# Decode attention plus MLP on one core: V in 4 MB transfers, P turned whole, the MLP's first half ahead of K

## The chip, the cores and the metric

One core of a Trainium2 chip runs the whole kernel in one launch. The metric is the device time of that launch in microseconds, lower is better. Engines are called PE (matrix), DVE (vector), ACT (scalar), POOL (GpSimd) and SP (sync); SP issues nearly all DMAs here, on one queue that is served by 16 DMA engines.

## The reference

```python
xn = layernorm(A_x)                                   # A_x: 4 x 1 x 576, bf16
out = A_x + attention(xn) + mlp(xn)

# attention: B=4, Hq=32, Hkv=16 (two query heads share a KV head), Dh=128, Sk=8192
W = 2048                                              # only the last 2048 keys of the cache
q = (xn @ wq).reshape(4, 1, 32, 128)                  # wq: 576 x 4096
p = softmax(q . k[:, :, Sk-W:] * 128**-0.5)
attention = (p . v[:, :, Sk-W:]).reshape(4, 1, 4096) @ wo      # wo: 4096 x 576

# mlp: h = gelu(layernorm(xn) @ w1) (576 x 576); four channel groups of h are shifted along S,
# where S = 1, so that the shifted entries are the zero padding; hs = shifted @ w2
x1 = xn + hs
mlp = x1 + gelu(layernorm(x1) @ w3) @ w4              # w3: 576 x 4608, w4: 4608 x 576
```

K and V of the window are 33.6 MB each; all weights together are 21.5 MB. Everything is read once.

## The kernel before

Each engine's program is a list of operations with a key; the list is sorted by key and written out in that order (`emit_program`). An operation names the signals that it waits for, so the keys set the order on an engine and the waits set the dependencies between engines. SP's list is the order of the DMAs: one that waits holds back all behind it.

**K stage.** 16 chunks, each one batch entry and four KV heads (`CH`), 2 MB, in 16 KB runs, loaded into a ring of ten slots. A chunk is 128 partitions (4 heads x 32 groups of 64 keys). PE transposes 64 tiles of 128 x 128 per chunk (`pe_T`, L333), eight to a PSUM bank (three banks, `NTB`); DVE (L340) and ACT (L339, blocks `ACT_EVAC`) copy them to `ktbuf`. `pe_SC` (L351) multiplies with the query: four matmuls of 512 columns at the four column positions 0, 32, 64, 96. The sixteen of a chunk are issued together. All scores of the four PSUM banks `Sps` accumulate over the chunks, so that the 128 rows are the 128 pairs of batch and query head.

**Softmax.** DVE takes the maximum (L372), ACT the exponentials (L376). P is then masked into four copies (L384), turned in 64 small matmuls (L393), copied (L402), permuted by a matmul (L404) and copied again (L406), on ACT.

**PV stage.** V comes in 16 chunks of 2 MB like K's. For each chunk DVE builds a padded, masked slice of P (`dve_pad`, L422), and PE runs 64 matmuls with a V tile as weights and 8 columns of P (L433). After a KV group's last chunk the rows are scaled (`OTn`, L472), selected (`sel`, L449) and multiplied with wo (`pe_AO`), in three portions (`AO_CH`).

**Weights.** wq loads first and K follows. w1, w2 and wo wait for the softmax and are issued after the eighth V chunk; wo in two DMAs with 4.6 KB runs. The MLP's first half runs in the PV stage. w3 (five DMAs) and w4 (five pieces of 18, 10, 5, 2 and 1 row per partition, `W4_ROWS`) come after V and reuse the ring. The h2 product (L525, L529: 180 matmuls with w3 as strided weights) runs near the end, and then the w4 product: 36 rows in two halves of 288 columns (L456, the helper `acc_mm`), both at column position 0, added in PSUM (`ACC`) to the residual and the attention's result. `fin0` and `fin1` (L550, L551) copy the sums out, and two DMAs write them.

Of the kernel before, what the change touches and what calls it, by code (L numbers as in the profile page):

```python
# [12 lines left out]
NSLOT = 10  # L13
NKT = 12
NTB = 3
SC_LAG = 2
ACT_EVAC = (1, 4, 7)
N_WARM = 6
AO_CH = ((0, 4), (4, 6), (6, 8))
# [14 lines left out]
def bass_parallel_sum__sliding_block_cached__mixer_s_mlp__decode_kernel(  # L34
# [8 lines left out]
    NU = 4  # L43
# [11 lines left out]
    CH = [(b, gq) for gq in range(4) for b in range(B)]  # L55
    x2 = A_x.rearrange("b s d -> (b s) d")
    o2 = out.rearrange("b s d -> (b s) d")

    with ExitStack() as ctx:
# [5 lines left out]

        ring_t = sb("ring", [128, NSLOT * UE], BF16)
        regB_t = sb("regB", [128, NKT * 1024], BF16)
        PT_t = sb("PT", [128, NT * 32], BF16)
# [4 lines left out]
        P4 = regB_t[:, 0:4 * NU * 512].rearrange("p (q t u i) -> p q t u i", q=4, t=16, u=NU)  # L73
        PTx = regB_t[:, 4 * NU * 512:4 * NU * 512 + 4 * 512].rearrange("p (q x) -> p q x", q=4)
        PTpad = regB_t[:, 0:2 * NT * 2 * NU].rearrange("p (s t u e) -> p s t u e", s=2, t=NT, u=NU)
        PTv = PT_t[:].rearrange("p (t c e) -> p t c e", t=NT, c=NC)

        wqmain = ring_t[:, 8 * UE:10 * UE].rearrange("p (r n) -> p r n", r=4)
        wqrag = PT_t[:, 0:Hq * Dh // 2]
        wo_a = ring_t[:, 4 * UE:4 * UE + 7 * 4 * D].rearrange("p (h r n) -> p h r n", h=7, r=4)  # L80
        _o = 2 * NT * 2 * NU
        wo_b = regB_t[:, _o:_o + 4 * D].rearrange("p (r n) -> p r n", r=4)
        _o += 4 * D
        w1main = regB_t[:, _o:_o + 4 * D].rearrange("p (r n) -> p r n", r=4)
        _o += 4 * D
        w1rag = regB_t[:, _o:_o + HALF]
        _o += HALF
        w2main = regB_t[:, _o:_o + 4 * D].rearrange("p (r n) -> p r n", r=4)
        _o += 4 * D
        w2rag = regB_t[:, _o:_o + HALF]  # L90
        _o += HALF
        assert _o <= NKT * 1024
        wo_at = lambda hg: wo_a[:, hg] if hg < 7 else wo_b
        w3r = [ring_t[:, 6 * UE + r * F:6 * UE + (r + 1) * F] for r in range(3)] + [ring_t[:, 8 * UE:8 * UE + F]]
        w3rag = ring_t[:, 6 * UE + 3 * F:6 * UE + 3 * F + FH]
        assert 3 * F + FH <= 2 * UE
# [9 lines left out]
        x1n_bf = sb("x1n_bf", [B, D], BF16)  # L106
        ragsrc = sb("ragsrc", [B, 3, 2, 128], BF16)
# [9 lines left out]
        permT_bf = sb("permT_bf", [128, 128], BF16)  # L117
        ident_f = sb("ident_f", [128, 128], FP32)
        ones_f = sb("ones_f", [128, 128], FP32)
        mask4 = sb("mask4", [128, NU], FP32)  # L120
        sel_f = sb("sel_f", [128, 32], FP32)
        sel_bf = sb("sel_bf", [128, 32], BF16)
        mU = sb("mU", [128, NU], FP32)
        mU_bf = sb("mU_bf", [128, NU, 2], BF16)
        diag = sb("diag", [128, 128], FP32)
        zeros_bf = sb("zeros_bf", [128, 512], BF16)
# [5 lines left out]
        rinvB = sb("rinvB", [128, 128], FP32)  # L132
        P_sb = Qpad_t[:, 0:2048].rearrange("p (q x) -> p q x", q=4)
        OTn = sb("OTn", [128, 128], BF16)
        ORT = sb("ORT", [128, 4, 8, B], BF16)
        t1 = sb("t1", [B, D], FP32)
        out_sb = x1n_bf
# [4 lines left out]
        PTps = [ps[:, 4 + k, :].rearrange("p (t x) -> p t x", t=16) for k in range(4)]  # L142
        ACC = [ps[0:B, k, 0:HALF] for k in range(2)]
        ORps = ps[:, 2, 0:128].rearrange("p (r h b) -> p r h b", r=4, h=8)
        rinvps = ps[:, 3, 0:128]
        OTps = [ps[:, 6 - max(gq - 1, 0), 0:128] for gq in range(4)]
        QTps = ps[:, 7, 0:128]
        HSps = ps[0:B, 7, 128:128 + HALF]
        HTps = ps[:, 7, 416:440].rearrange("p (c b) -> p c b", b=B)
        XTps = [ps[:, 7, 440 + 12 * k:452 + 12 * k].bitcast(BF16).rearrange("p (c b) -> p c b", b=B) for k in range(3)]  # L150
        H2Tps = ps[:, 7, 0:144].rearrange("p (c b) -> p c b", b=B)
# [25 lines left out]

        KS = float(NB + 4)
# [6 lines left out]
        def pool_ident(t, tag, pattern, view, key):  # L185
# [3 lines left out]
        P(lambda e: e.memset(zeros_bf[:], 0.0), sig="zeros_bf", key=-100)  # L189
# [4 lines left out]
        pool_ident(permT_bf, "permT_bf", [[-1, NI], [-NI, NU]], permT_bf[:].rearrange("p (i u) -> p i u", u=NU), -95)  # L194
        pool_ident(ident_f, "ident_f", [[-1, 128]], ident_f[:], -94)
        P(lambda e: e.memset(hs_inT[:], 0.0), sig="hs_inT", key=-90)
        P(lambda e: e.memset(ones_f[:], 1.0), sig="ones_f", key=-89)


        add("dve", lambda e: e.tensor_reduce(out=mask4[:], in_=ident_f[:].rearrange("p (u x) -> p u x", u=NU), axis=AX.X, op=ALU.add),  # L200
            waits=["ident_f"], sig="mask4", key=-8)
        add("dve", lambda e: e.tensor_reduce(out=sel_f[:], in_=ident_f[:].rearrange("p (u x) -> p x u", u=NU), axis=AX.X, op=ALU.add),
            waits=["ident_f"], sig="sel_f", key=-8)
        add("dve", lambda e: e.tensor_copy(out=sel_bf[:], in_=sel_f[:]), waits=["sel_f"], sig="sel_bf", key=-7.9)
        add("dve", lambda e: e.tensor_reduce(out=mU[:], in_=ident_f[:].rearrange("p (i u) -> p u i", u=NU), axis=AX.X, op=ALU.add),
            waits=["ident_f"], sig="mU", key=-8)
        for x in range(2):
            add("dve", lambda e, x=x: e.tensor_copy(out=mU_bf[:, :, x], in_=mU[:]), waits=["mU"], sig=f"mU_bf{x}", key=-7.8)
# [3 lines left out]
        ev_wq = [add_dma([(ring_t[:, 8 * UE:10 * UE], A_wq[0:512, :].rearrange("(p r) n -> p (r n)", r=4))], "wq", (), -20),  # L212
                 add_dma([(wqrag, rag_src(A_wq))], "wqr", (), -15)]

        def kv_src(cache, c):
            b, gq = CH[c]
            return cache[b, NU * gq:NU * gq + NU, Sk - W:Sk, :].rearrange("g (i t) d -> i g (t d)", t=NT)

        k_slot = lambda c: c % NSLOT
        v_slot = lambda c: (6, 7, 8, 9, 0, 1, 2, 3)[c % 8]  # L220
        t_done = lambda c: f"T{NBLK * c + NBLK - 1}"
        ev_k, ev_v = [], []
        for c in range(NC):
            w = ["q"] if c in (8, 9) else ([t_done(c - NSLOT)] if c >= NSLOT else [])
            ev_k.append(add_dma([(slot(k_slot(c)), kv_src(A_k_cache, c))], ("ring", k_slot(c)), w, c))
        for c in range(NC):
            w = [f"PV{c - 8}"] if c >= 8 else [t_done(c + 6)]
            ev_v.append(add_dma([(slot(v_slot(c)), kv_src(A_v_cache, c))], ("ring", v_slot(c)), w, KS + c))
            if c == 7:
                free = ["PTy3"]  # L230
                ev_w1 = add_dma([(w1main, B_w1[0:512, :].rearrange("(p r) n -> p r n", r=4)), (w1rag, rag_src(B_w1))], "w1",
                                free, KS + c + 0.1)
                ev_w2 = add_dma([(w2main, B_w2[0:512, :].rearrange("(p r) n -> p r n", r=4)), (w2rag, rag_src(B_w2))], "w2",
                                free, KS + c + 0.2)
                wo_s = A_wo.rearrange("(h p r) n -> p h (r n)", h=8, r=4)
                ev_wo = add_dma([(wo_a.rearrange("p h r n -> p h (r n)"), wo_s[:, 0:7, :]),
                                 (wo_b.rearrange("p r n -> p (r n)"), wo_s[:, 7, :])],
                                "wo", [t_done(NC - 1)] + free, KS + c + 0.3)
        w3_src = B_w3[0:512, :].rearrange("(p r) n -> p r n", r=4)
        ev_w3 = [add_dma([(w3r[r], w3_src[:, r, :])], ("w3", r), ["PV10" if r == 3 else "PV9"], KT + r) for r in range(4)]  # L240
        ev_w3.append(add_dma([(w3rag, rag_src(B_w3))], ("w3", 4), ["PV9"], KT + 4))
        w4tile, w4cols, ev_w4, W4N = [], [], [], []
        base = 0
        offs = (8 * UE + F, 0, 10 * D, 15 * D, 17 * D)
        assert F + 18 * D <= 2 * UE and 18 * D <= 2 * UE
        for n, rc in enumerate(W4_ROWS):
            v = ring_t[:, offs[n]:offs[n] + rc * D]
            ev_w4.append(add_dma([(v, B_w4[base:base + 128 * rc, :].rearrange("(p r) n -> p (r n)", r=rc))], ("w4", n),
                                 ["PV11" if n == 0 else "PV13"], KT + 5 + n))
            W4N.append((len(w4tile), len(w4tile) + rc))  # L250
            for r in range(rc):
                w4tile.append(v[:, r * D:(r + 1) * D])
                w4cols.append((base + r, base + 128 * rc, rc))
            base += 128 * rc
        assert len(w4tile) == 36 and base == F
        ev_o = [None, None]
        for h, eng in ((0, "sp"), (1, "act")):
            ev_o[h] = add_dma([(o2[:, HALF * h:HALF * (h + 1)], out_sb[:, HALF * h:HALF * (h + 1)])], ("out", h),
                              [f"fin{h}"], 10000, engine=eng)
            add(eng, lambda e: None, [ev_o[h]], None, 10001)  # L260


        def ln_ops(idx, src, dst, first_waits, tag, k0):
# [11 lines left out]
            add("dve", lambda e: (e.tensor_copy(out=ragsrc[:, idx, 0, 0:128:2], in_=dst[:, 512:D]),  # L275
# [81 lines left out]
        for n in range(NB):  # L357
            w = [ev_k[n // NBLK]] if n % NBLK == 0 else []
            if n == 0:
                w.append("perm_bf")  # L360
# [271 lines left out]
```

## Time and profile before

| | us |
|---|---|
| median of 3 runs | 224.17 |
| lowest, highest | 224.01, 224.96 |
| the profiled execution, span from first to last instruction | 222.3 |
| PE busy | 162.3 (73%) |
| DVE busy | 76.9 (35%) |
| ACT busy | 61.2 (28%) |
| transposes of K on PE, L333 | 66.7 |
| w4 product, L456 | 11.1 |
| HBM read | 88.49 MB, 398 GB/s over the span |

The profiled execution has no time of its own in the record beside its span; the span is 1.9 us under the median of the runs, which includes what lies before the first and after the last instruction. The page's slices are 5.56 us each; a digit is the busy share in tenths. PEclk is the clock granted to PE: full until slice 19, about half from slice 20 on. In the groups, a line gives engine, operation, operands, count, then busy time, the mean duration of one in ns, and the engine's idle time ahead of it. Matmuls overlap, so the distance between two starts is shorter than the duration of one.

### The profile page before, as it was taken

Reading aid. Unit: us, or ns where it says so; the run is one execution under the profiler, and the core shown is the slowest. Engines: PE = TensorE matmul, PEld = TensorE weight load, DVE = VectorE, ACT = ScalarE, POOL = GpSimd, SP = SyncE. Lnnn points to the kernel's source line nnn. Section 1 sums busy time; section 2 is a strip of 40 time slices with the busy share of each in tenths; the row PEclk is TensorE's granted clock in tenths of the full one; section 3 lists DMA queues with packets and bytes.
Section 4 is the critical chain, followed back from the end, with each engine's and each line's share of the span. In section 5 each row is a group of like instructions: output and inputs, shape, how many; then the busy total and the mean of one; then the engine's idle time right before and its main releaser. Section 6 shows DMA issues by size and latency. Waiting matters only on the chain.

```text
span 222.3 us, 6311 instructions
## 1 busy us (share of the span) xinstructions
PE 162.3 (73%) x2964; PEld 126.4 (57%) x2966; DVE 76.9 (35%) x162; ACT 61.2 (28%) x75; POOL 5.5 (2%) x17
## 2 busy tenths in 40 slices
PE   0068999999999999995377653001948996699596
PEld 0065777777777777773257653001545584489363
DVE  4303656666666655666822111000150010000000
ACT  2000655556556665555860000000002000000000
POOL 8100000000000000000000000000000000000000
PEclk9999999999999999999655555555555697585589
DMA  7999999999999999999999999999999999999820
GB/s 284 407 410 425 436 431 419 420 428 431 428 431 422 422 431 428 423 422 422 425 428 425 433 405 401 413 438 428 428 425 419 428 431 415 421 426 428 359 109 1
DMA packets 8017, 88.90 MB, mean 400 GB/s; under 512 B 812, under 2 KB 1208, under 8 KB 3000
## 3 DMA queue, kind: packets, MB, share of 16 engines
q1 hardware_dynamic: 7976, 88.50, 94.7%
q8 instruction: 23, 0.38, 0.7%
q14 instruction: 2, 0.02, 0.0%
q10 hardware_dynamic: 16, 0.01, 0.0%
HBM read 88.49 MB, written 0.00 MB: 398 GB/s over the span
## 4 chain that ended last, share of the span: by engine, by line
DMA 56%; PE 41%; ACT 1%; issue 1%; SPq 1%; DVE 0%
DMA ring<-in_A_v_cache_dram 34%; PE ps L333 25%; DMA ring<-in_B_w_dram 16%; PE ps L351 6%; DMA ring<-in_A_wq_dram 6%; PE ps L456 5%; PE ps L304 2%; PE ps L433 2%; PE ps L321 1%; ACT regB L339 1%; SPq L171 1%; DVE Qpad L313 0%; ACT x1n_bf L551 0%; PE ps L283 0%; PE ps L286 0%
## 5 line engine op out<-in xcount | busy, mean ns | idle before, releaser
L333 PE MATMUL ps<-perm_bf,ring 128*128 128x128 bf16 x1024 | 66.7, 221 | 0.5 <-ACT regB L339 0.4
L333 PEld LDWEIGHTS ps<-perm_bf,ring 128*128 128x128 bf16 x1024 | 58.0, 98 | 13.5 <-issue 6.9
L340 DVE COPY regB<-ps 128x1024 bf16<-128x1024 bf16 x80 | 52.3, 687 | 29.9 <-PE ps L333 28.1
L339 ACT ACTIVATE regB<-ps 128x1024 bf16<-128x1024 bf16 x48 | 47.5, 1022 | 48.8 <-PE ps L333 48.8
L433 PE MATMUL ps<-regB,ring 128*128 128x8 bf16 x1024 | 29.0, 168 | 33.8 <-DMA ring<-in_A_v_cache_dram 27.8
L433 PEld LDWEIGHTS ps<-regB,ring 128*128 128x128 bf16 x1024 | 28.3, 103 | 37.1 <-issue 31.8
L351 PE MATMUL ps<-regB,Qpad 128*32 128x512 bf16 x256 | 16.9, 382 | 0.4 <-ACT regB L339 0.4
L269 ACT ACTIVATE sd<-mv 4x1 f32<-4x1 f32 x3 | 0.6, 202 | 51.1 <-DVE mv L267 51.1
L456 PE MATMUL ps<-ring,h2T_sb 128*4 128x288 bf16 x72 | 11.1, 325 | 2.3 <-DMA ring<-in_B_w_dram 2.3
L422 DVE TENSOR_TENSOR regB<-PT,mU_bf 128x512 bf16<-128x512 bf16 x16 | 6.6, 419 | 15.9 <-PE ps L433 13.8
L456 PE MATMUL ps<-ring,ORT 128*4 128x288 bf16 x56 | 11.3, 380 | 0.3 <-DVE ORT L475 0.3
L535 ACT ACTIVATE h2T_sb<-ps 128x144 bf16<-128x144 f32 x1 | 0.3, 292 | 37.3 <-PE ps L529 37.3
L456 PEld LDWEIGHTS ps<-ring,h2T_sb 128*4 128x4 bf16 x72 | 6.8, 95 | 6.3 <-DMA ring<-in_B_w_dram 2.4
L475 DVE CAST ORT<-ps 128x32 bf16<-128x32 f32 (+1 forms) x3 | 0.6, 203 | 26.7 <-PE ps L449 26.7
L550 DVE CAST x1n_bf<-ps 4x288 bf16<-4x288 f32 x1 | 0.4, 446 | 27.0 <-PE ps L456 27.0
L304 PE MATMUL ps<-xnT,ring 128*128 128x4 bf16 x128 | 3.6, 166 | 7.9 <-DMA ring<-in_A_wq_dram 7.9
L351 PEld LDWEIGHTS ps<-regB,Qpad 128*32 128x32 bf16 x256 | 5.3, 95 | 6.0 <-issue 0.9
L456 PEld LDWEIGHTS ps<-ring,ORT 128*4 128x4 bf16 x56 | 5.8, 107 | 4.5 <-DVE ORT L475 0.4
L525 PEld LDWEIGHTS ps<-x1nT,ring 128*128 128x128 bf16 x144 | 8.0, 152 | 0.2 <-issue 0.2
L525 PE MATMUL ps<-x1nT,ring 128*128 128x4 bf16 x144 | 8.1, 194 | 0.0
L304 PEld LDWEIGHTS ps<-xnT,ring 128*128 128x128 bf16 x128 | 3.5, 104 | 7.9 <-DMA ring<-in_A_wq_dram 7.9
L472 DVE TENSOR_TENSOR OTn<-ps,rinvB 128x32 bf16<-128x32 f32 (+1 forms) x3 | 0.6, 202 | 18.5 <-PE ps L433 18.5
(92 smaller groups left out, 72.3 us busy)
## 6 DMA issues: line engine op xcount, KB each, us to landing
ring<-in_A_k_cache_dram SPq DMA_DIRECT2D x16, 2048.0 KB, 43.3
ring<-in_A_v_cache_dram SPq DMA_DIRECT2D x16, 2048.0 KB, 43.1
ring<-in_B_w_dram SPq DMA_DIRECT2D x4, 1152.0 KB, 33.4
ring<-in_A_wq_dram SPq DMA_DIRECT2D x1, 4096.0 KB, 12.3
ring<-in_A_wo_dram SPq DMA_DIRECT2D x1, 4032.0 KB, 32.1
ring<-in_B_w_dram SPq DMA_DIRECT2D x1, 2592.0 KB, 36.6
ring<-in_B_w_dram SPq DMA_DIRECT2D x1, 1440.0 KB, 30.3
regB<-in_B_w_dram SPq DMA_DIRECT2D x2, 576.0 KB, 21.3
```

What stands on the lines that cost most here:

```text
L171: e.dma_start(o_, i_).then_inc(S[skey], 16)
L269: add("act", lambda e: e.activation(out=sd[:, idx:idx + 1], in_=mv[:, idx, 1:2], func=ACTF.Sqrt, bias=EPS, scale=1.0), waits=[f"{tag}_mv"] ...
L304: ins = e.matmul(QTps[:, B * h:B * (h + 1)], lhsT=w, rhs=x_, start=(r == 0 and h == 0), stop=(r == 4), skip_group_check=True)
L321: ins = e.matmul(ps[:, 4 + (w % NTB), :], lhsT=zeros_bf[:, 0:128], rhs=zeros_bf[:, :], start=True, stop=True)
L333: ins = e.transpose(tb[n % NTB][:, t, :], slot_t(k_slot(c))[:, 8 * k + t, :], perm_bf[:])
L339: return "act", lambda e: e.activation(out=ktbuf[:, n % NKT], in_=tb[n % NTB], func=ACTF.Copy)
L340: return "dve", lambda e: e.tensor_copy(out=ktbuf[:, n % NKT], in_=tb[n % NTB])
L351: ins = e.matmul(Sps[32 * u:32 * u + 32, q, :].rearrange("p (t i) -> p t i", t=16), lhsT=Qpad_t[:, qo:qo + 32], rhs=ktgrp[:, s % (NKT // 2 ...
L422: return lambda e: e.tensor_tensor(out=PTpad[:, c % 2], in0=PTv[:, :, cc, :].unsqueeze(2).to_broadcast([128, NT, NU, 2]), in1=mU_bf[:].uns ...
L433: ins = e.matmul(o_, lhsT=slot_t(v_slot(c))[:, t, :], rhs=PTpad[:, c % 2, t].rearrange("p u e -> p (u e)"), start=(t == 0), stop=(t == NT ...
L456: return e.matmul(ACC[h], lhsT=lhsT, rhs=rhs, start=start, stop=stop)
L525: ins = e.matmul(H2Tps[:, n, :], lhsT=w3r[r][:, lo:hi:st], rhs=x1nT[:, r, :], start=(r == 0 and n == 0), stop=False, skip_group_check=True)
```

## The change

- **V**: 8 transfers of 4 MB in place of 16 of 2 MB. Chunk c takes the KV heads m, m+4, m+8, m+12 (m = c // 2) of all four batch entries, and the half j = c % 2 of each run of 256 keys: 128 partitions of 32 KB runs. The last chunk comes in two halves. V uses the K ring as four slots.
- **P**: turned whole in 16 matmuls of 128 columns (`pe_PT`) and copied by DVE to `PTn`. For each V chunk, 16 matmuls of 256 columns with a 0/1 matrix `Sel` spread it over partitions (`pe_B`), and eight DVE products mask it into `PTpad` (`dve_pad`). A PV matmul has 32 columns instead of 8, and all chunks of two m share one accumulation.
- **Order**: w1, w2 and w3 load right after wq, ahead of K, into places of their own (w3: `regX`) or into the ring; the MLP up to h2 runs before the first transpose. K has a ring of 8 slots, four PSUM banks and eight places in `ktbuf`; score matmuls are issued in fours, one group for each two blocks.
- **wo**: two groups of four DMAs, each DMA for 32 partitions with 18 KB runs, in `regX` where w3 was; group 0 is issued ahead of V3, group 1 ahead of V6.
- **Output**: the halves of the wo and w4 products go to the column positions 0 and 32 (`ACC`, `tile_position=(0, 32 * h)`). `OTn`, the transposed `OTT`, the masked `OTm` and eight `sel` matmuls replace the old selection; the wo product has two portions.
- The maximum is taken bank by bank, and the programs are written out without `nc.Block`.

```diff
-NSLOT = 10
-NKT = 12
-NTB = 3
-SC_LAG = 2
+NSLOT = 8
+NKT = 8
+NTB = 4
+SC_LAG = 3
...
-        ACC = [ps[0:B, k, 0:HALF] for k in range(2)]
+        ACC = [ps[0:B, 0, 0:HALF], ps[32:32 + B, 1, 0:HALF]]
...
+        ev_w1 = add_dma([(w1main.rearrange("p r n -> p (r n)"), main_src(B_w1)), (w1rag, rag_src(B_w1))], "w1", (), -14)
+        ev_w2 = add_dma([(w2main.rearrange("p r n -> p (r n)"), main_src(B_w2)), (w2rag, rag_src(B_w2))], "w2", (), -13)
+        ev_w3 = add_dma([(w3main, main_src(B_w3)), (w3rag, rag_src(B_w3))], "w3", (), -12)
...
+        def v_src(c, lo, hi):
+            m, j = c // 2, c % 2
+            v = A_v_cache[:, m:Hkv:4, Sk - W:Sk, :].rearrange("b k (i j t) d -> j (b k) i t d", j=2, t=VT)[j]
+            return v[:, :, lo:hi, :].rearrange("g i t d -> g i (t d)")
...
-            w = ["q"] if c in (8, 9) else ([t_done(c - NSLOT)] if c >= NSLOT else [])
+            w = {4: ["q"], 5: ["q"], 6: ["q", "hT", "x1"], 7: ["q", "hT", "x1"]}.get(c, [])
+            if c >= NSLOT:
+                w = [t_done(c - NSLOT)]
...
+        def wo_dma(g, key):
+            pairs = []
+            for k in range(4):
+                r0 = 1024 * k + 512 * g
+                pairs.append((wo_h[g][32 * k:32 * k + 32, :], A_wo[r0:r0 + 512, :].rearrange("(p r) n -> p (r n)", r=16)))
+            ev_wo.append(add_dma(pairs, ("wo", g), ["h2_4"], key))
+        for c in range(VC):
+            s = c % 4
+            w = [f"PV{c - 4}"] if c >= 4 else [t_done(2 * c + 9)]
+            if c == 3:
+                wo_dma(0, KS + c - 0.1)
+            if c == 6:
+                wo_dma(1, KS + c - 0.1)
+            if c < VC - 1:
+                ev_v.append([add_dma([(vslot(s), v_src(c, 0, VT))], ("vring", s), w, KS + c)])
+            else:
+                ev_v.append([add_dma([(vslot(s)[:, VE // 2 * k:VE // 2 * (k + 1)], v_src(c, VT // 2 * k, VT // 2 * (k + 1)))],
+                                     ("v7", k), w, KS + c + 0.1 * k) for k in range(2)])
...
-                                 ["PV11" if n == 0 else "PV13"], KT + 5 + n))
+                                 ["PV4" if n == 0 else "PV5"], KT + 5 + n))
...
+            if n == 0:
+                w += ["perm_bf", "gelu_h"]
...
-                key=8 * (s // 4) + 7 + SC_LAG + 0.5)
+                key=2 * s + 1 + SC_LAG + 0.5)
...
+                    ins = e.matmul(PBps[n % 2][:, 256 * k:256 * k + 256],
+                                   lhsT=Sel[:, a].rearrange("p u i -> p (u i)"),
+                                   rhs=PTn[:, :, 2 * j:2 * j + 2, 32 * m:32 * m + 32], start=True, stop=True, skip_group_check=True)
...
+                out=PTpad[:, c % 2, 2 * n:2 * n + 2].rearrange("p a k x -> p (a k) x"),
+                in0=PBps[n % 2].rearrange("p (a x) -> p a x", x=32),
+                in1=mU_bf[:].rearrange("p u e -> p (u e)").unsqueeze(1).to_broadcast([128, 16, 32]), op=ALU.mult)
...
+                    ins = e.matmul(o_, lhsT=vslot_t(c % 4)[:, t, :], rhs=PTpad[:, c % 2, a, k, :],
+                                   start=(j == 0 and first), stop=(j == 1 and last))
...
+        def acc_mm(e, h, lhsT, rhs, stop=False):
+            return e.matmul(ACC[h], lhsT=lhsT, rhs=rhs, start=False, stop=stop, tile_position=(0, 32 * h), skip_group_check=True)
...
-        with nc.Block() as block:
...
+        for nm, engine in (("sp", nc.sync), ("pool", nc.gpsimd), ("dve", nc.vector), ("act", nc.scalar), ("pe", nc.tensor)):
+            emit_program(nm, engine)
```

## The prediction

> **What bounds the kernel now.** I read the page's slices and queue table first, to see which resource never rests:
>
> ```profile
> DMA  7999999999999999999999999999999999999820
> ...
> DMA packets 8017, 88.90 MB, mean 400 GB/s; under 512 B 812, under 2 KB 1208, under 8 KB 3000
> ...
> q1 hardware_dynamic: 7976, 88.50, 94.7%
> ```
>
> The DMA row is 9 from the second slice to slice 37: the engines never wait for a buffer, through the score stage, the softmax or the PV stage. So PE, DVE and ACT matter only where they make DMA wait, or after it has finished. The table by stretch (span of the stretch, busy us and instructions of PE, PEld, DVE, ACT, POOL, then granted clock, DMA share, GB/s) shows where it finishes:
>
> ```profile
> 50.00:92.00 42.00, 41.94 (x666) 32.60 (x664) 27.51 (x43) 24.56 (x26) 0.00 (x0) 1.00 1.01 427
> ...
> 206.00:209.00 3.00, 0.72 (x17) 0.64 (x16) 0.00 (x0) 0.29 (x1) 0.00 (x0) 0.50 0.95 398
> 209.00:212.00 3.00, 3.00 (x13) 1.60 (x14) 0.00 (x0) 0.00 (x0) 0.00 (x0) 0.50 0.65 261
> 212.00:215.00 3.00, 3.00 (x21) 1.86 (x19) 0.00 (x0) 0.00 (x0) 0.00 (x0) 0.78 0.38 151
> 215.00:222.30 7.30, 5.08 (x42) 3.31 (x39) 0.45 (x1) 0.40 (x1) 0.00 (x0) 1.00 0.00 1
> ```
>
> Some of the 16 DMA engines run dry at 209.5, the last lands its w4 bytes at 214.8 (the trace's packet records). The chain of waits names what comes after:
>
> ```profile
> 172.33 36.62 DMA ring<-in_B_w_dram
> 208.95 0.04 issue
> 208.99 11.10 PE ps L456 x72
> 220.09 0.02 issue
> 220.12 0.40 ACT x1n_bf L551
> ```
>
> So the span is 214.8 us of DMA and a tail of 7.5 us: 72 w4 matmuls of 288 columns, one after the other, 240 ns apart while the granted clock is 0.50 and 122 ns apart after 213.3. The rows I price with:
>
> ```profile
> L333 PE MATMUL ps<-perm_bf,ring 128*128 128x128 bf16 x1024 | 66.7, 221 | 0.5 <-ACT regB L339 0.4
> ...
> L351 PE MATMUL ps<-regB,Qpad 128*32 128x512 bf16 x256 | 16.9, 382 | 0.4 <-ACT regB L339 0.4
> ...
> L525 PE MATMUL ps<-x1nT,ring 128*128 128x4 bf16 x144 | 8.1, 194 | 0.0
> ...
> L393 PE MATMUL ps<-sel_bf,regB 128*128 128x32 bf16 x64 | 2.4, 189 | 5.5 <-DVE regB L384 5.4
> ```
>
> Median packet durations in the trace: 576 B 29 ns, 1152 B 51, 4608 B 182, 9216 B 351, 16384 B 613, 32768 B 1221. That is 5 ns plus 27 bytes per ns, on each of 16 engines.
>
> **The tail (L456, ACC).** The two halves of each w4 row go to column groups 0 and 32. L351 shows what column groups do: four 512-column matmuls start within 10 ns of each other and the next four 216 ns later, so they run side by side. Then a pair costs what one matmul does now: 36 pairs take 4.4 us at clock 1.0, 8.6 at 0.50, in place of 11.1. The first w4 piece lands some 6 us before the last, so most pairs run while DMA still moves. After the last byte: 0.45 to reach PE (208.50 to 208.95 now), 0.7 for the last small pieces and some backlog at the low clock (bounds 0.15 and 4), 0.45 for fin, 1.85 from there to the span's end (220.45 to 222.3). Sum 3.4 instead of 7.5: -4.1. Removing the Block takes at most the 0.4 SP waits at its end; I take -0.4.
>
> **Bytes.** The same 88.5 MB. V: 2048 packets x 613 / 16 = 78.5 us becomes 896 x 1221 + 256 x 613 over 16 = 78.2: -0.3. w3: 512 x 351 / 16 = 11.2, becoming 128 packets of 36 KB at 1373 = 11.0: -0.2. Bigger runs buy almost nothing, as 16 KB packets already move 26.7 bytes per ns. For V the unseen thing is the address pattern: 16 heads 8 MB apart rather than 4 heads 2 MB apart. From below it is these 78.2 us (contiguous 32 KB packets of wq took 1221); the slowest 32 KB row is wq's first packets, 1938 ns at the 95th percentile, 1.6 times, +46 us. I take 1221, the nearest, and keep a small chance for more.
>
> [...]
>
> **wo is the term that decides.** Now each wo DMA spans 128 partitions: 1024 packets x 182 / 16 = 11.6 us. After, each of eight DMAs writes 32 partitions only, two 18 KB rows for each engine. At the rate above: 256 x 689 / 16 = 11.0, so -0.6. But every large packet in this trace went to a 128-partition tile, where each engine has eight partitions to itself. All move 27 bytes per ns, and whether that is the engine's limit or that of the partitions' side can't be read from it. If it is the partitions', 16 engines crowd onto a quarter of them: 2x if two engines share an entry, 4x if four do: 22.0 or 44.1 us, +10.4 or +32.5. The nearest row is x_sb, four rows of 1152 B on four partitions: 72, 60, 48 and 56 ns against 51, so 1.0 to 1.4x, though packets this small can hide in a buffer. I take 2x, the geometric middle, and less 1.0 because engines end 5 us apart (209.5 to 214.8), so sharers are not all in step: +9.4. Both ends stay in the range, the upper with little weight.
>
> [...]
>
> Nothing hides this: wo stands in SP's queue ahead of V3 and V6, and the DMA row has no gap to absorb it.
>
> **What moves to the front, and its cover.** wq, w1, w2, w3 load ahead of K: 13.9 + 2 x (128 x 182 + 128 x 29) / 16 = 17.3, + 11.0 + 1.5 = 29.8 us. Their PE work but h2 lies under w3's landing. h2 is 180 matmuls at 56 ns (L525: 144 in 8.06) = 10.1, then the warm-up 2.5: the first transpose starts near 43, now 21. Per K chunk, 64 transposes 56 ns apart are 3.58; a lone group of four score matmuls costs 0.415 with the switch both ways (93 ns in, 322 out), so four are 1.66 where a batch of 16 costs 1.07 now; the 0.40 us waiting for ACT's copies goes with the fourth bank. Sum 5.3 against 5.05 now. K ends at 43 + 16 x 5.3 + 2 = 130. Then maximum, four exps (0.66 apart), turn, B and pad of chunk 0 (512 f32 from PSUM, about 0.65 on DVE by L372's 1.1 ns an element; eight of them) and PV0: 15.5, so PV0 ends near 145.5. PV's 32-column matmuls cost 28 ns (L393), B 0.1 to 0.2 each: 5.3 to 7 us a chunk, under V's 9.8.
>
> Who waits: SP's V4 waits for PV0, and everything later is queued behind it. DMA has work until 29.8 + 78.4 (K) + 29.3 (V0 to V2) + 5.5 (wo) + 9.8 (V3) = 152.8, or 158 with slow wo. The cover is 7 us or more: cost nothing. If K chunks took 5.8, it would be used up. The added waits elsewhere cost nothing either: gelu2 stands ahead of ACT's first copies but waits for h2_4 near 40.5, before T0 runs; SC1 to SC3 wait for x1 and gelu2, ready by then; wo's DMAs wait for h2_4, w4's for PV4 and PV5, both done before SP reaches them; POOL's memset of OTn waits for h2_4 with nothing queued behind it.
>
> **Sum.** Span 222.3 - 4.1 - 0.4 - 0.3 - 0.2 + 9.4 = 226.7. The median of the runs, 224.17, stands 1.9 over the span of the profiled execution: 228.6.
>
> **Rivals.**
> *wo at full rate* (the engine is the limit): -0.6 in place of +9.4, span 216.7, 218.6 us. For it: x_sb's packets. Against: four packets of 1 KB test no sustained rate. This ends on the other side; the point of balance is wo at 1.45x.
> *Half the loss*: the engines' lag lets about half the sharing pairs pass each other: wo +4.7, 223.9.
> *Slow V or a starved queue*: V's 32 KB packets 10% longer add 7.8 to the forecast: 236; or K chunks past 6.2 us (clock 0.50 for a part of the stage) make V4 late by some us. For it: the address pattern is new. Against: DMA ran at 427 GB/s with every pattern so far.
> That the bigger runs speed up DMA is ruled out by the packet rows: 0.5 us.
>
> **How the numbers follow.** Forecast 0.50, full rate 0.27, half the loss 0.13, slow V or starved 0.10. About 0.5% (1.1 us) is what a measurement can tell from no change. Full rate is faster; half the loss spreads 0.02, 0.06, 0.05 over faster, same, slower; the others are slower: 0.29, 0.06, 0.65. The range reaches from the full-rate case, 218.0, to 233, the forecast with 4 us of clock or V trouble. The likeliest case alone: 226 to 231.
>
> **What would show it.** Right: about ten us in which DMA engines are full by share while GB/s falls to 200 to 250, near 137 to 148 and again near 175 to 190 (wo's 18 KB packets at 1.3 us, not 0.69); pairs of w4 matmuls 122 to 240 ns apart; last landing near 224; first transpose near 43 and 5.3 a chunk; DMA at 9 throughout. Wrong: wo's packets at 0.69 (then 218.6); V's packets well over 1.22; a gap in the DMA row before V4; a tail over 5 us.

## The result, and the profile after

The changed kernel takes 312.99 us in the median of four runs (310.96 to 314.96), the kernel before 224.09 us (223.14 to 224.96): a ratio of 1.396, with an interval of 1.389 to 1.404. The forecast was 228.6, and its range ended at 233.0. The profiled execution took 312.62 us, with a span of 311.3.

The page of the changed kernel, its slices and its queue table:

```profile
span 311.3 us, 6418 instructions
...
DMA  8999999999999999999999999999999999899981
GB/s 316 393 444 421 425 425 427 429 423 423 427 425 427 396 199 223 225 213 206 213 219 199 229 208 221 202 219 202 226 215 194 226 206 213 194 221 239 261 370 77
DMA packets 5906, 88.90 MB, mean 286 GB/s; under 512 B 748, under 2 KB 1144, under 8 KB 1912
...
q1 hardware_dynamic: 5864, 88.50, 97.1%
```

The DMA row alone would look healthy, as before: 9 nearly everywhere. The row under it shows the trouble. A slice is 7.8 us; from slice 15 on, near 109 us, the same full engines move some 195 to 240 GB/s where they moved 425. The bytes are the same 88.5 MB. So the engines did not wait for buffers; each of V's packets took twice as long. The stretches say it again (span of the stretch, busy time and instructions of PE, PEld, DVE, ACT, POOL, granted clock, DMA share, GB/s):

```profile
45.00:87.00 42.00, 42.00 (x637) 31.80 (x635) 26.97 (x41) 24.13 (x24) 0.00 (x0) 1.00 1.00 425
...
140.00:300.00 160.00, 56.37 (x1204) 44.35 (x1201) 45.78 (x75) 0.00 (x0) 0.00 (x0) 0.63 1.00 220
300.00:305.00 5.00, 4.42 (x44) 2.62 (x46) 0.43 (x2) 0.00 (x0) 0.00 (x0) 0.55 0.76 306
305.00:311.30 6.30, 4.35 (x72) 2.83 (x66) 0.45 (x1) 0.40 (x1) 0.00 (x0) 1.00 0.11 43
```

The K stage runs at the full 425 GB/s, the V stage at half of that, with PE busy for a third of it. By the packet records, V's 32 KB packets took 2467 ns in the median (wq's, of the same size and in the same kernel, 1221); the last V chunk's 16 KB packets 1153 ns (K's: 614); wo's 18 KB packets 1393 ns; the first w4 packets, which run beside the end of V, 1055 ns (774 in the kernel before). Divided by 16 engines: V 157.0 us, wo 22.3, that w4 piece 8.8. All packets together come to 302.4 us, 92.0 more than the 210.4 of before. The last packet of w4 ends at 308.63 us, against 214.81.

The groups name who waited for it:

```profile
L510 PE MATMUL ps<-regB,ring 128*128 128x32 bf16 x1024 | 37.8, 185 | 100.4 <-DMA ring<-in_A_v_cache_dram 92.1
...
L544 PE MATMUL ps<-ring,h2T_sb 128*4 128x288 bf16 x72 | 4.6, 286 | 0.0
```

L510 is the PV product: of its 100.4 us of idle time 92.1 were spent waiting for V. L544 is w4: 72 matmuls in 4.6 us where L456 of before was busy for 11.1, with no idle time ahead of them. A part of this is the clock: here all 72 ran at a granted clock of 1.00, in the kernel before some at 0.50. At 122 ns each, 72 in a row would take 8.8 us, so side by side they take about half. That part did what it was meant to.

### The profile page after: what moved, and what is told of

Its sections match the earlier page's. It is cut to its first block, busy times and chain, and to the rows that moved or that the text cites. A ratio compares the mean times of both kernels' runs of the same rounds, so it can differ in the third digit from the quotient of the medians.

```text
span 311.3 us, 6418 instructions
## 1 busy us (share of the span) xinstructions
PE 176.7 (57%) x3011; PEld 135.2 (43%) x3012; DVE 116.0 (37%) x210; ACT 57.3 (18%) x66; POOL 4.8 (2%) x17
## 4 chain that ended last, share of the span: by engine, by line
PE 41%; another core or an unknown queue 28%; DMA 24%; issue 3%; DVE 2%; SPq 1%
PE ps L410 16%; DMA ring<-in_A_v_cache_dram 15%; DMA regX<-in_B_w_dram 9%; PE ps L510 8%; PE ps L490 5%; PE ps L427 5%; PE ps L544 3%; PE ps L391 3%; SPq L176 1%; DVE regB L497 1%; PE ps L349 1%; PE ps L395 1%; DVE regX L577 0%; PE ps L555 0%
## 5 line engine op out<-in xcount | busy, mean ns | idle before, releaser
L510 PE MATMUL ps<-regB,ring 128*128 128x32 bf16 x1024 | 37.8, 185 | 100.4 <-DMA ring<-in_A_v_cache_dram 92.1
L510 PEld LDWEIGHTS ps<-regB,ring 128*128 128x128 bf16 x1024 | 37.7, 104 | 103.8 <-DMA ring<-in_A_v_cache_dram 94.1
L497 DVE TENSOR_TENSOR regB<-ps,mU_bf 128x512 bf16<-128x512 f32 x64 | 42.3, 691 | 105.1 <-PE ps L490 104.6
L490 PE MATMUL ps<-PTn,Sel 128*128 128x256 bf16 x128 | 32.2, 348 | 1.6 <-DVE rsum L474 0.9
L427 PE MATMUL ps<-regB,Qpad 128*32 128x512 bf16 x256 | 26.2, 400 | 0.9 <-DVE rmax L450 0.9
L391 PE MATMUL ps<-x1nT,regX 128*128 128x4 bf16 x144 | 8.1, 194 | 7.5 <-DMA regX<-in_B_w_dram 7.5
L490 PEld LDWEIGHTS ps<-PTn,Sel 128*128 128x128 bf16 x128 | 8.3, 102 | 8.7 <-issue 3.9
L391 PEld LDWEIGHTS ps<-x1nT,regX 128*128 128x128 bf16 x144 | 8.0, 152 | 7.6 <-DMA regX<-in_B_w_dram 7.6
L544 PE MATMUL ps<-regX 128*4 128x288 bf16 x64 | 5.9, 354 | 1.1 <-DVE regX L582 1.1
L544 PEld LDWEIGHTS ps<-regX 128*4 128x4 bf16 x64 | 3.2, 102 | 3.4 <-DVE regX L582 1.4
L544 PE MATMUL ps<-ring,h2T_sb 128*4 128x288 bf16 x72 | 4.6, 286 | 0.0
```

Of the source, the lines that this page charges most:

```text
L391: ins = e.matmul(H2Tps[:, n, :], lhsT=w3r[r][:, lo:hi:st], rhs=x1nT[:, r, :], start=(r == 0 and n == 0), stop=False, skip_group_check=True)
L427: ins = e.matmul(Sps[32 * u:32 * u + 32, q, :].rearrange("p (t i) -> p t i", t=16), lhsT=Qpad_t[:, qo:qo + 32], rhs=ktgrp[:, s % (NKT // 2 ...
L490: ins = e.matmul(PBps[n % 2][:, 256 * k:256 * k + 256], lhsT=Sel[:, a].rearrange("p u i -> p (u i)"), rhs=PTn[:, :, 2 * j:2 * j + 2, 32 * ...
L497: return lambda e: e.tensor_tensor(out=PTpad[:, c % 2, 2 * n:2 * n + 2].rearrange("p a k x -> p (a k) x"), in0=PBps[n % 2].rearrange("p (a ...
L510: ins = e.matmul(o_, lhsT=vslot_t(c % 4)[:, t, :], rhs=PTpad[:, c % 2, a, k, :], start=(j == 0 and first), stop=(j == 1 and last))
L544: return e.matmul(ACC[h], lhsT=lhsT, rhs=rhs, start=False, stop=stop, tile_position=(0, 32 * h), skip_group_check=True)
```

## The experiments

Two explanations for V's packets were in the foreground. **Addresses**: the 16 heads that one transfer reads lie 8 MB apart, and the engines, in step, meet in the same part of HBM. **Places**: the order in which the rows of a transfer are handed to engines makes several engines write the same part of SBUF at a time. K's transfers, and V's before, read their source as 32 rows of 4 ("i g", 32x4); the changed V reads it as 16 rows of 8 (16x8), and wo goes to 32 partitions a transfer.

**m1_patterns.** The loads alone, twelve patterns one after the other, each complete before the next starts. The first, A, is the changed V's; C is A with 4 KB more between heads, D with 64 KB more; E has heads 2 MB apart, F 4 MB; B hands out the same rows as 8x16; G and J are other 8x16 patterns; H and I are 16 KB rows as 4x32 and as 16x8; W1 and W2 are wo as one transfer of 4x32 rows, and as it is in the changed kernel.

> Loads alone, nothing computed, the output is zeros. Twelve phases one after the other, 8.4 MB each (wo: 4.7 MB), differing in the address pattern of the rows. Theory A (rows of heads 8 MB apart that the 16 DMA engines read at one moment cost HBM half its rate): the changed kernel's V pattern (A) takes about 2450 ns for each 32 KB packet and 40 us for the phase; a head pitch of 8 MB plus 4 KB or plus 64 KB (C, D), otherwise the same, about 1220 ns and 21 us; heads 2 MB and 4 MB apart (E, F) in between; eight heads with 16 neighbouring runs each (G, J) and four heads with 32 runs of 16 KB (H) near the full 27 bytes per ns. Sixteen heads with 16 KB runs (I): half rate again. Theory B (32 KB packets, or 4 MB transfers, or three-level source patterns are slow): A to G and J all near 2450, C and D as slow as A, I and H full. wo on 128 partitions (W1): 689 ns a packet, 11 us; on 32 partitions (W2): 1390 ns and 22 us by the theory that engines share the partitions' side, 689 ns if wo was slow in the kernel only because V's rows were read beside it.

Eight of the twelve, as stretches of the profile (span of the stretch, busy POOL, clock, DMA share, GB/s), in the order A, B, C, E, H, I, W1, W2:

```profile
2.20:43.60 41.40, 0.00 (x0) 1.00 0.97 202
45.80:124.20 78.40, 0.00 (x0) 1.00 0.50 107
126.20:167.40 41.20, 0.00 (x0) 1.00 0.96 202
211.90:252.90 41.00, 0.00 (x0) 1.00 0.97 202
461.70:559.70 98.00, 0.00 (x0) 1.00 0.25 86
561.90:601.60 39.70, 0.00 (x0) 1.00 0.98 211
603.80:675.10 71.30, 0.00 (x0) 1.00 0.24 66
676.70:700.30 23.60, 0.00 (x0) 1.00 0.94 200
```

A is slow with nothing else running, 2545 ns a packet. Every change of the addresses left it there: 4 KB of skew (C) 202 GB/s, 64 KB of skew 208, heads 4 MB apart 203, 2 MB apart (E) 202. The theory of addresses fell. The size of packets and transfers (theory B) is not the cause either: I, with 16 KB rows in 2 MB transfers, took 1246 ns a packet where K's took 613. The DMA share tells a second thing, which I had not priced: it is 0.50 for patterns whose outer count is 8 (B, and G and J at some 106 GB/s), and 0.25 for 4, so H, G, J and W1 all missed what was expected of them. The shares of 0.25 (0.24 in W1), 0.50 and 0.97 for outer counts of 4, 8 and 16 fit four, eight and all of the 16 engines at work. W2 shows wo slow by itself: 1428 ns a packet, 23.6 us.

**e1_wo128.** The changed kernel with wo in one transfer per group onto all 128 partitions.

```diff
-            for k in range(4):
-                r0 = 1024 * k + 512 * g
-                pairs.append((wo_h[g][32 * k:32 * k + 32, :], A_wo[r0:r0 + 512, :].rearrange("(p r) n -> p (r n)", r=16)))
+            src = A_wo.rearrange("(k g p r) n -> g k p (r n)", k=4, g=2, p=32, r=16)[g]
+            ev_wo.append(add_dma([(wo_h[g], src)], ("wo", g), ["h2_4"], key))
```

> The changed kernel with wo in one DMA per group onto 128 partitions; same bytes, same 18 KB runs. If the 32-partition target costs: wo's packets fall from 1393 to 689 ns, wo from 22.3 to 11.0 us and the time from 313 to about 302. If wo was slow because of V's rows beside it: packets stay near 1390 and the time within 2 us of 313. V's packets stay at 2457 in both.

364.06 us: a miss. The source begins with k = 4, as W1's did at a DMA share of 0.24, and here the share falls to 0.21 at the end: most of the engines stand idle. Its packets stayed at 1406 ns beside the slow V, so the run says nothing about the 32 partitions. The page's DMA row:

```profile
DMA  8999999999999999999999999999999877322220
```

The stretch from 315 us on, with DMA share and GB/s last:

```profile
315.00:362.00 47.00, 19.83 (x385) 14.74 (x385) 7.12 (x12) 0.40 (x1) 0.00 (x0) 0.63 0.21 79
```

**e4_vig.** e1_wo128 with V's rows handed out as 8x16 (run outside, head inside), the masks following.

```diff
-            v = A_v_cache[:, m:Hkv:4, Sk - W:Sk, :].rearrange("b k (i j t) d -> j (b k) i t d", j=2, t=VT)[j]
-            return v[:, :, lo:hi, :].rearrange("g i t d -> g i (t d)")
+            v = A_v_cache[:, m:Hkv:4, Sk - W:Sk, :].rearrange("b k (i j t) d -> j i (b k) t d", j=2, t=VT)[j]
+            return v[:, :, lo:hi, :].rearrange("i g t d -> i g (t d)")
...
```

> [...] If the rows that are in flight together decide: V's packets come down from 2457, to between 1221 and 1900 ns, and the time to between 222 and 270. If a row pitch of 8 MB costs in any order, or the packet size does: V's packets stay at 2457 and the time at about 302.

450.31 us: a miss for the same reason, the share that m1_patterns showed for an outer count of 8 (120 to 350 us: DMA share 0.50, 136 GB/s); V's packets came down only to 1937 ns in the median. Both runs speak for a rule on the order, but against my idea that any order other than 16x8 would do.

**e6_before_v16.** The kernel before, its 2 MB transfers and 16 KB packets unchanged, but V read from 16 heads as 16x8.

```diff
+            m, j = c // 4, c % 4
+            v16 = A_v_cache[:, m:Hkv:4, Sk - W:Sk, :].rearrange("b k (i j t) d -> j (b k) i (t d)", j=4, t=NT)[j]
-            ev_v.append(add_dma([(slot(v_slot(c)), kv_src(A_v_cache, c))], ("ring", v_slot(c)), w, KS + c))
+            ev_v.append(add_dma([(slot(v_slot(c)), v16)], ("ring", v_slot(c)), w, KS + c))
```

> The kernel before with V read from 16 heads 8 MB apart, 8 runs of 16 KB each, in place of 4 heads 2 MB apart with 32 runs; same packet size, same 2 MB transfers. It multiplies P with other V rows than the reference. If the addresses decide: V's 16 KB packets go from 613 to about 1200 ns and the time from 224 to about 300. If packet or transfer size decides: 613 and 224.

298.22 us, 74 over the kernel before, with V packets of 1147 ns in the median in place of 613. A stretch of it (DMA share and GB/s last):

```profile
100.00:200.00 100.00, 29.03 (x728) 23.55 (x729) 15.01 (x38) 12.70 (x21) 0.00 (x0) 0.54 1.01 252
```

So neither the 4 MB transfers, nor the 32 KB runs, nor the new PV stage is needed for the loss; the 16x8 source alone makes it.

**m2_ports.** The loads alone again, 32 KB rows: (a) 32x4, (b) 64x2, (c) 16x8 from neighbouring rows, (d) the same rows as one list of 128, (e, f, g) 16 rows of 4, 2 and 1 onto the first 64, 32 and 16 partitions, (h, i) 16x8 after a transfer meant to hold up 4 or 8 of the engines, (w) wo as 32x4. The theories are again places and addresses.

> Loads alone again, output zeros, 32 KB rows throughout. [...] Rival (addresses): rows far apart in HBM are slow to read. Rival (pattern): a 16 x 8 pattern is slow for another reason, in whatever state the engines are. Phase a, 32 x 4 rows, heads 4 MB apart: places 1220 ns a packet, 20 us for 8.4 MB; addresses 2450. [...] c, 16 x 8 rows that lie nearly one after the other: places 2450, addresses 1220. d, 128 rows one after the other: 1220 in all. [...] w, wo as 32 x 4 rows: 689 ns and 11 us.

Stretches a, c, d, e, f, g and w, with columns as in m1_patterns:

```profile
2.20:23.90 21.70, 0.00 (x0) 1.00 0.91 385
48.90:89.30 40.40, 0.00 (x0) 1.00 0.97 203
91.10:111.50 20.40, 0.00 (x0) 1.00 0.96 405
113.30:153.70 40.40, 0.00 (x0) 1.00 0.97 207
155.60:177.40 21.80, 0.00 (x0) 1.00 0.93 191
179.40:199.50 20.10, 0.00 (x0) 1.00 0.93 104
380.00:392.00 12.00, 0.00 (x0) 1.00 0.96 393
```

c and d settle it between addresses and the order of rows: nearly neighbouring rows in both, the same 128 partitions, 16 engines busy in both, and 203 against 405 GB/s. So do a and m1's F: heads 4 MB apart in both, 385 GB/s as 32x4, 203 as 16x8 (b, as 64x2, reached 390). e, f and g write fewer partitions: onto 64, 32 and 16, 16 engines reach 207, 191 and 104 GB/s, packets of 2466, 2561 and 4815 ns. e and f also begin with 16, so by themselves they don't part place from order; g, with one row for each engine, does, and so does W2, a plain list of 32 rows onto 32 partitions at 200 GB/s. The 16x8 order over 128 partitions lands at the rate of a transfer onto 64 (203 and 207 GB/s). If engines that meet because they run in step made the loss, h, which was to hold up four of them by four packets, should have sped up, and it did not (204 GB/s, 2514 ns; i 201). Which engine writes which partition is not in the trace. So the order as cause is shown; that it acts through the places is inferred and open.

**e7_wo_p4.** The changed kernel with wo alone mended: rows as 32x4, partition 4p + k, with the selection matrix Z permuted to match.

```diff
...
+            src = A_wo.rearrange("(k g p r) n -> g p k (r n)", k=4, g=2, p=32, r=16)[g]
+            ev_wo.append(add_dma([(wo_h[g], src)], ("wo", g), ["h2_4"], key))
...
```

> The changed kernel with wo in one DMA per group as 32 x 4 rows onto 128 partitions, partition 4p + k in place of 32k + p, and the selection matrix to match; V as in the change. Places: wo's packets 689 ns on 16 engines in place of 1393, time 313 - 11 = 302. If wo was slow because of V's rows beside it: packets above 1000 ns and 308 to 313.

305.88 us: 7 us gained of the 11 hoped for. wo's packets took 1271 ns in the median, though the fastest took 686. The packets fit the rival, the time lies between the two: the slow V packets still run beside wo's, and a good transfer next to a bad one is slow as well.

**e8_v32.** e7_wo_p4 with V read from every second head, 32 heads of 4 runs, still 4 MB and 32 KB a run.

```diff
-            v = A_v_cache[:, m:Hkv:4, Sk - W:Sk, :].rearrange("b k (i j t) d -> j (b k) i t d", j=2, t=VT)[j]
+            v = A_v_cache.rearrange("b h s d -> (b h) s d")[m % 2::2, Sk - W:Sk, :].rearrange("g (i j t) d -> j g i t d", i=4, t=VT)[2 * (m // 2) + j]
```

> As the run with wo as 32 x 4 rows, and V's 4 MB from 32 heads 4 MB apart, four 32 KB runs of each, 32 x 4 rows in place of 16 x 8. It multiplies P with other V rows than the reference; all else is unchanged. Places: V's packets 1221 ns in place of 2457, V 78 us in place of 156, and the time near 218 (the forecast's full-rate rival, 218.6). Addresses: 2450 and about 302. [...]

219.57 us. V's packets took 1215 ns, wo's 688, and the GB/s row stays near 425 up to the end:

```profile
GB/s 271 408 391 467 432 393 426 423 432 423 426 429 426 432 426 423 429 420 426 462 413 435 426 429 424 408 450 429 432 429 423 411 436 434 402 430 437 402 252 17
```

With two orders of rows changed, 93 us are gone, and the time is near the 218.6 of the rival "wo at full rate".

**e11_v32_only.** e8_v32 with wo back on 32 partitions a transfer: the case that the forecast had thought likeliest.

> The changed kernel with V alone mended (32 heads x 4 runs of 32 KB, dealt 32x4, other V rows than the computation wants); wo stays on 32 partitions a transfer. This is the case that the prediction took as likeliest: V's packets 1215 ns, wo's about 1390 with 22 us for 4.7 MB, time e8_v32 plus 9.4 us, 229 (227 to 231). Rival (wo's packets are slow only beside a slow V): wo's packets near 700 ns and 220 us.

237.44 us: beyond both. wo's packets took 1332 ns, 20.7 us by 16 engines, where the forecast had 21.0 (22.0 less 1.0); this is 9.6 over e8_v32. But 105 of the 32 KB packets (12 in e8_v32) took over 1820 ns, 2287 in the median, most of them V's beside wo's, and the 32 KB packets together took 7.1 us more. The two make 16.7 of the 16.8 us by which the packet time of an engine rose. Two stretches, beside wo and between:

```profile
137.00:152.00 15.00, 11.18 (x192) 7.62 (x192) 10.58 (x18) 0.00 (x0) 0.00 (x0) 0.73 1.04 231
155.00:175.00 20.00, 15.05 (x307) 11.48 (x304) 11.43 (x18) 0.00 (x0) 0.00 (x0) 0.67 0.99 425
```

**e5_before_wo32.** The kernel before with wo cut into transfers of 32 partitions.

```diff
+                wo_d = wo_a.rearrange("p h r n -> p h (r n)")
+                wo_e = wo_b.rearrange("p r n -> p (r n)")
+                qs = [slice(32 * q, 32 * q + 32) for q in range(4)]
+                ev_wo = add_dma([(wo_d[q], wo_s[q, 0:7, :]) for q in qs] + [(wo_e[q], wo_s[q, 7, :]) for q in qs],
...
```

> The kernel before with wo's two transfers cut into four each of 32 partitions. [...] Rival (wo's slow packets in the changed kernel come from the 18 KB runs): 224 to 225.

237.39 us, some 14 over the kernel before, where 10 were expected (234: wo's 11.6 us at half the rate). The 4608 B packets of wo took 358 ns (182 before), 11.5 us more in sum; the rest is again the neighbours, 75 of the 16 KB packets (20 before) at 1114 ns, 2.0 us more than before. So the 18 KB runs are not needed for wo's loss: transfers of 32 partitions make it here too. The slow stretch stands out in the middle of a fast kernel:

```profile
135.00:157.00 22.00, 1.85 (x64) 1.79 (x64) 0.55 (x2) 0.00 (x0) 0.00 (x0) 0.50 1.04 218
160.00:180.00 20.00, 8.56 (x225) 6.76 (x226) 4.23 (x13) 0.20 (x1) 0.00 (x0) 0.50 1.01 405
```

**e9_v2mb.** The changed kernel with the whole computation and both orders mended: V in 16 transfers of 2 MB, four heads of one batch, handed out as K's. The turned P then needs four spreading matmuls and one masked product for each chunk, and PV matmuls of 8 columns.

```diff
...
+            return A_v_cache[b, m:Hkv:4, Sk - W:Sk, :].rearrange("k (i t) d -> i k (t d)", t=NT)
...
+                    ins = e.matmul(PBps[c % 2][:, 128 * a:128 * a + 128], lhsT=Sel[:, a].rearrange("p i u -> p (i u)"),
+                                   rhs=PTn[:, :, :, 32 * m + 8 * b:32 * m + 8 * b + 8], start=True, stop=True, skip_group_check=True)
...
```

> The changed kernel with the whole computation, V in 16 transfers of 2 MB (4 heads of one batch, 32 runs of 16 KB each, dealt 32x4, as K's), P spread by 4 matmuls of 128 columns and one masked product per chunk, wo as 32x4 rows. Theory (the order in which rows go to partitions sets the rate, not run or transfer size): V's packets 614 ns, wo's 688, the loads end as in e8_v32, 219.5 us (217.5 to 221.5), so about 0.98 of the kernel before. Rival (4 MB transfers with 32 KB runs are themselves worth something): V at the rate of the kernel before but slower than e8_v32 by the 0.3 us of bytes per packet and more, 221 to 224.

218.34 us (218.04 to 219.04), 0.978 of the kernel before with an interval of 0.976 to 0.980: faster than the kernel before by about 2%, and far faster than the changed one. From its page:

```profile
span 216.7 us, 6252 instructions
...
q1 hardware_dynamic: 6776, 88.50, 96.7%
...
L485 DVE TENSOR_TENSOR regB<-ps,mU_bf 128x512 bf16<-128x512 f32 x16 | 11.1, 692 | 51.6 <-PE ps L479 51.6
```

The masked product is 16 instructions of 692 ns, and DVE stood idle 51.6 us waiting for PE ahead of them. Its stretches:

```profile
140.00:200.00 60.00, 38.36 (x999) 31.37 (x998) 11.06 (x19) 0.00 (x0) 0.00 (x0) 0.53 1.01 426
...
210.00:216.70 6.70, 4.66 (x70) 2.60 (x66) 0.45 (x1) 0.40 (x1) 0.00 (x0) 1.00 0.27 106
```

The transfers are half as large as e8_v32's and the time is 1.2 us less (one run there), so large transfers and long runs bought nothing that shows in the time. In the loads they bought 0.4 us: the last w4 packet ends at 213.69 us in e8_v32 and at 214.07 here, and the stretch behind it is 4.6 us there and 2.6 here. Against the kernel before the last packet is 0.74 us earlier; the other 4.8 us of the 5.6 by which the span is shorter lie behind it.

**e10_tail.** e9_v2mb with both halves of the output in the array's columns 0 to 31.

```diff
-        ACC = [ps[0:B, 0, 0:HALF], ps[32:32 + B, 1, 0:HALF]]
+        ACC = [ps[0:B, k, 0:HALF] for k in range(2)]
...
-            return e.matmul(ACC[h], lhsT=lhsT, rhs=rhs, start=False, stop=stop, tile_position=(0, 32 * h), skip_group_check=True)
+            return e.matmul(ACC[h], lhsT=lhsT, rhs=rhs, start=False, stop=stop, tile_position=(0, 0), skip_group_check=True)
...
```

> e9_v2mb with both halves of the output accumulated in the PE array's columns 0 to 31 (as in the kernel before) in place of 0 to 31 and 32 to 63. Theory (the prediction's tail term, 4.1 us): the pairs of w4 matmuls run one after the other, 240 ns a pair and more in place of 122, the stretch from the last w4 packet to the end of the span grows from about 3 us to 6 to 7, time 3 to 4.5 us over e9_v2mb. Rival (the end of the last packet alone sets the tail): the same as e9_v2mb within 0.7 us.

224.46 us (223.62 to 225.08), 1.003 of the kernel before (1.002 to 1.005): the whole gain of e9_v2mb is gone, and more. It is 6.1 us over e9_v2mb, where 3 to 4.5 were expected, which fits the last part of the wo product running one after the other too. The ends of the two chains of waits, first e9_v2mb's, then e10_tail's:

```profile
181.01 32.39 DMA ring<-in_B_w_dram
213.44 1.41 PE ps L508 x16
```

```profile
202.06 1.88 PE ps L497 x64
206.32 15.43 PE ps L508 x104
```

With column groups the chain stays with DMA until 213.4 us and leaves 16 matmuls; without them the chain is PE's from 206 on, with 104 matmuls (the last wo group and w4) one after the other. The last w4 packet ends at the same time in both (214.05 and 214.07); the stretch behind it is 9.5 and 2.6 us. The rival, that the end of the last packet alone sets the tail, is refuted.

## Why the prediction was wrong, step by step

**What bounds the kernel**: right. DMA never rests, before and after, and the time follows the packets: 92.0 us more of packet time per engine, 93.8 us later for the last packet, 4.8 us less behind it, sum 89.0.

**The step that failed** is the price of V's packets under "Bytes": "I take 1221, the nearest". They took 2467 ns, one of the signs that the prediction had named for being wrong; V came to 157.0 us, not 78.2, and 78.8 of the 84.6 us that the span of 226.7 was short are this one term. The nearest row by size was not the nearest by what mattered. wq's rows and K's were a list of 128 and a 32x4 order; 16x8 occurred nowhere in the trace. I asked where the rows come from and never who writes them where, although I asked just that for wo a paragraph later and found the right size. V's transfers fill 128 partitions, and I took that to mean that they spread. The diff showed it: in "j (b k) i t d", behind the index j, the first count is that of "b k", 16.

**The addresses**, which I had called the unseen thing, are not the reason. Heads 2 MB apart, 8 MB apart and with 4 KB more all gave 202 GB/s, and neighbouring rows 203, while heads 4 MB apart as 32x4 gave 385.

**wo**: right in size, 22.3 us in the changed kernel against 22.0 for the full 2x. That writing 32 partitions costs this by itself is shown by W2 and e5_before_wo32; in the changed kernel the slow V beside wo is a second cause, as e7_wo_p4 shows. That two engines share an entry, as the 2x had it, no run shows, nor whether x_sb's small packets hide in a buffer; the runs show how long the packets took, 1393 ns in the changed kernel and 1428 in W2 against 688 in e8_v32. But the sum around it was short. I took 1.0 off because engines out of step might pass each other; e11_v32_only shows the opposite, 7.1 us added, as V's packets beside wo's are slowed too. So even with V at full rate the kernel takes 237.4 (one run, e11_v32_only), not 228.6, and the range would have missed it.

**The tail**: the mechanism is right: the two w4 matmuls of a pair start 1 to 3 ns apart and the next pair 122 ns later, and e10_tail shows that this carries the whole gain of e9_v2mb. The size, 2.7 us against 3.4 in the changed kernel, is in part luck. With V at full rate (e8_v32, e11_v32_only) the stretch was 4.6 and 5.1 us, as the chain of waits ends there with 8.1 and 8.7 us of PE work on wo and w4: what the sum had at 0.7 us was about 1.9 and 2.4. The 0.4 us taken for the Block can't be told apart from this.

**The front and its cover**: right where it could be seen. The first transpose started at 44.0 us (forecast 43), a K chunk took 5.32 (5.3). PV0 ended near 152, not 145.5: the last K chunk and the clock, 0.88 between 100 and 140 us, were late. DMA had no gap, as V's slow packets stretched the cover. In e8_v32 and e9_v2mb, with fast packets, the DMA row shows no gap either, so the cover holds.

**The range.** The rival "slow V" had the right place and a size of 10%, picked without a row. The one row I had named, wq's first packets, gave +46 us, and I left it out of the range with the case's chance at 0.10. An order of rows that no trace shows should have had twice the packet, the factor I took for wo, in the price of that rival.

## What to carry to other kernels

Judge a transfer by its source pattern, not by its bytes: with outermost counts of 4, 8 and 16 the DMA share was 0.25, 0.50 and 0.97 here, and 16 rows of 8 onto 128 partitions ran at half the rate of 32 rows of 4 (203 against 385 GB/s), with the engines busy in both (0.97 and 0.91). Read GB/s beside the DMA share: 1.00 at 220 GB/s and 1.00 at 425 are the same row of nines, and a packet's median duration by size found the culprit at once (V's 2467 ns beside wq's 1221). Where 16 KB packets already run at full rate, longer runs buy next to nothing (0.4 us here); look behind the last byte, where two column groups were worth 6.1 us (224.46 against 218.34).

## What the runs showed of the hardware that I had not expected

The loss spreads to neighbours: with wo on 32 partitions, some 90 of V's well ordered 32 KB packets took 2287 ns instead of 1215, and in the changed kernel w4's first packets took 1055 ns instead of 774. The low rate of 16x8 does not depend on row size (2547 ns for 32 KB, 1246 for 16 KB), on addresses (202 GB/s with heads 2 and 8 MB apart), or on a transfer ahead that was meant to hold up a part of the engines (204 and 201 GB/s). A 4x32 order of 16 KB rows, at a DMA share of 0.25, had packets of 616 ns in the median, close to K's 613, though some took up to twice that: its 86 GB/s come in the main from the three quarters of the engines' time that are idle.
